# Windowed attention and channel mix on one core: every engine's order and engine choices re-planned, units 0 and 1's q and k loaded ahead

## The chip, the cores and the metric

The kernel runs on one core of a Trainium2 chip. The metric is the device time of one execution in microseconds (us). PE is the matrix engine, DVE the vector engine, ACT the scalar engine, POOL the GpSimd engine, and SP the engine whose queue issues nearly all DMAs here. Each of them works through its own list of instructions strictly in the order in which the program gave it; semaphores make an instruction wait for the work of another engine.

## What is computed

Two steps follow each other. First causal attention over 4 batches, 8 heads, 768 positions and 64 columns a head, where each position sees the 128 latest positions and the first 4 ("sinks"). Its result, with the heads put side by side (512 columns), is the x of an RWKV channel mix.

```python
keep = (pos[None, :] < 4) | ((rel >= 0) & (rel < 128))
a = softmax(where(keep, q @ k.T / 8, -1e9));  attn = a @ v
x = attn.transpose(0, 2, 1, 3).reshape(B, S, 512)
x_prev = x shifted by one position
xk = mu_k * x + (1 - mu_k) * x_prev
xr = mu_r * x + (1 - mu_r) * x_prev
kk = relu(xk @ w_k) ** 2              # 512 -> 1024
out = sigmoid(xr @ w_r) * (kk @ w_v)  # 1024 -> 512
```

All inputs and the output are float32. The kernel multiplies in bf16 and accumulates in float32.

## The kernel before, in words

The work is cut into 12 units of 256 positions: unit u is third `u % 3` of batch `u // 3`. For each unit these stages follow one another, each written as a few operations that one engine does:

- load (L281 to L341): two DMAs of 256 KB each for k, q and v. Those of v (L304), of k from unit 4 and of q from unit 8 on (L314) move rows of 256 bytes; k and q of the earlier units come in rows of 1 KB (L334). The weights come in five DMAs of 1 MB (L351).
- prepare (L514 to L690): a cast of k and q to bf16 (L533, L540; tiles `kb`, `qb`), then a transpose to `kt` and `qt`. k of units 4 to 11 and q of units 8 to 11 are transposed by a DMA of the SP queue (L559); the others on PE (L573), and ACT or DVE copies the result out of PSUM (L586). v is cast to `vb` (L643). The four keys that all positions see are set aside by POOL (`ksink`, L667) and by PE and DVE (`vsink`, L673, L677).
- attend: scores on PE (`sc`, L718), exponential on ACT (`e`, L772), mask by a DVE product (L786), values on PE (`o`, L805; the sink part L693, L700, L760), reciprocal and scaling on DVE (`rec` L819, `x` L822).
- mix (L831 on): x is transposed on PE and copied out (L846, L855), or for units 9 to 11 by a DMA (L866); DVE forms the difference to the position before (`td`, L874) and `xk` and `xr` (L885).
- ffn (L928 on): `xk @ w_k` on PE (L936), relu on ACT or DVE (L946, L950), square on ACT or DVE (L964, L960), `xr @ w_r` on PE with a tanh on ACT (L976, L982), `kk @ w_v` on PE (L994), the gate on DVE (L1003) and the store by SP (L1010). Of the last unit's second half the product and the store are cut in two (L906, L916, L921).

The weights are cast to bf16 in pieces of 128 by 1024 (L498, L502, L504).

None of this is scheduled by the compiler. `Plan.op` only records an operation with its engine; `Plan.run` (L172) then emits all of them in the order of a list of numbers, `ORDER`. Three tables were worked out ahead of time: `ORDER`, in which an entry of 0 or more is an operation and a negative one is a product of zeros into a spare PSUM bank (`P.fill`, L1014: it keeps PE at work and computes nothing); `CHOICE`, which for operations that can be done by several engines names one that is not the default; and `SLOTS`, which buffer of its pool each tile takes. Only the order within each engine counts, since the engines run side by side. The pools are small: three buffers each for raw k, q and v and for raw weights, four for `kt` and `qt`, two pairs of PSUM banks for scores and four single ones for everything else on PE. An operation on one engine that stands ahead of others and waits for a load or for a buffer holds up all that stand behind it on that engine, and a DMA on the SP queue that waits for its source holds up the loads behind it.

Of the kernel before, what the change touches and what calls it, by code (L numbers as in the profile page):

```python
# [18 lines left out]
    90: "ACT", 91: "ACT", 92: "ACT", 93: "ACT", 95: "ACT", 97: "ACT", 99: "ACT", 100: "DVE",  # L19
    103: "DVE", 108: "DVE", 109: "POOL", 111: "DVE", 112: "ACT", 113: "ACT", 139: "DVE", 142:  # L20
    "DVE", 144: "DVE", 145: "DVE", 148: "DVE", 151: "DVE", 154: "DVE", 196: "POOL", 199: "POOL",
    202: "POOL", 206: "DVE", 223: "DVE", 227: "DVE", 228: "ACT", 278: "DVE", 283: "DVE", 284:
    "POOL", 287: "ACT", 288: "DVE", 300: "DVE", 309: "ACT", 313: "ACT", 320: "DVE", 356: "DVE",
    358: "POOL", 363: "POOL", 366: "ACT", 367: "ACT", 369: "DVE", 389: "ACT", 446: "DVE", 447:
    "ACT", 527: "DVE", 548: "ACT", 552: "ACT", 555: "DVE", 560: "ACT", 595: "DVE", 597: "DVE",
    600: "POOL", 602: "DVE", 605: "ACT", 606: "DVE", 628: "ACT", 636: "ACT", 677: "POOL", 681:
    "DVE", 683: "DVE", 684: "DVE", 702: "ACT", 706: "ACT", 710: "ACT", 714: "ACT", 753: "DVE",
    759: "DVE", 761: "ACT", 782: "DVE", 783: "ACT", 787: "ACT", 791: "ACT", 795: "ACT", 832:
    "DVE", 838: "ACT", 839: "ACT", 859: "ACT", 866: "DVE", 867: "ACT", 906: "POOL", 912: "DVE",
    914: "ACT", 915: "DVE", 931: "ACT", 935: "ACT", 939: "ACT", 943: "ACT", 1000: "DVE", 1004:  # L30
    "DVE", 1005: "ACT", 1008: "DVE", 1009: "ACT", 1028: "DVE", 1037: "ACT",
# [116 lines left out]
class Plan:  # L148
# [23 lines left out]
    def run(self):  # L172
        keys = [(name, key) for o in self.ops for name, key in o["take"]]
        for (name, key), slot in zip(keys, SLOTS, strict=True):
            self.buf[key] = self.pools[name][slot]
# [8 lines left out]
def kernel(  # L184
# [14 lines left out]
    nc = tc.nc  # L199
# [14 lines left out]
    P = Plan()  # L214
# [854 lines left out]
```

## Time and profile before

| | |
|---|---|
| three runs | 167.48, 169.1 and 170.65 us, median 169.1 us |
| span of the profiled execution | 167.6 us |
| busy: PE, DVE, ACT, POOL | 159.7, 146.2, 133.4, 16.6 us |
| granted PE clock | full speed in every slice |
| bytes | 24.12 MB read from memory, 6.29 MB written |
| products of zeros | 44, the last three from 20.77 us on |
| last product on PE ends | 163.9 us |

The profile has no separate figure for the profiled execution beyond its span of 167.6 us, which lies 0.1 us above the fastest of the three runs and 1.5 us under their median. "Busy" of PE runs to the modelled end of each product, and products are pipelined: one of 512 columns is shown with some 380 ns, while in a row of four each takes 215 ns. So PE's share says when it had nothing at all, not how fast it went; the chain of waits shows the rows without the overlap. DVE and ACT overlap too, by less: a following instruction starts some 80 to 120 ns before the one ahead of it is shown to end.

### The profile page before, as it was taken

The numbers are of one execution on the slowest core, as the hardware profiler recorded it, in microseconds if no ns is written. First come the engines' busy times: TensorE is split into PE (matmuls) and PEld (weight loads), VectorE is DVE, ScalarE is ACT, GpSimd is POOL, SyncE is SP. The second block draws the span as 40 slices with busy tenths as digits, with TensorE's granted clock in tenths as the row PEclk, the third lists the DMA queues.
The fourth block names the chain that finished last, engine by engine and source line by source line (L and its number), as shares of the span: only waits on it lengthen the run. The fifth ranks groups of instructions, "written<-read, shape, count | busy, mean of one in ns | idle before, by whom it ended". The sixth has DMA issues, their size and how long they took to land.

```text
span 167.6 us, 4210 instructions
## 1 busy us (share of the span) xinstructions
PE 159.7 (95%) x1601; PEld 102.4 (61%) x1601; DVE 146.2 (87%) x375; ACT 133.4 (80%) x221; POOL 16.6 (10%) x43
## 2 busy tenths in 40 slices
PE   6999997999999999899999999999999999999991
PEld 1447574755558576676556885665765576764850
DVE  5189999999999999899999999989798799998821
ACT  4269998999999997999879999989799829614340
POOL 6423021005000010022000000010010000000000
PEclk9999999999999999999999999999999999999999
DMA  4999989999899999979999999999997774131303
GB/s 102 300 327 369 346 172 312 372 324 328 189 248 166 204 294 224 253 153 133 218 256 149 214 239 174 233 219 200 211 189 185 194 162 155 63 66 63 125 0 125
DMA packets 79042, 34.60 MB, mean 206 GB/s; under 512 B 67112, under 2 KB 73520, under 8 KB 79024
## 3 DMA queue, kind: packets, MB, share of 16 engines
q1 hardware_dynamic: 79008, 34.35, 92.0%
q8 instruction: 12, 0.20, 0.5%
q14 instruction: 6, 0.05, 0.1%
q10 hardware_dynamic: 16, 0.00, 0.0%
HBM read 24.12 MB, written 6.29 MB: 181 GB/s over the span
## 4 chain that ended last, share of the span: by engine, by line
PE 58%; DVE 11%; DMA 11%; SPq 7%; ACT 7%; issue 3%; ACTq 0%; DVEq 0%
PE bank L936 18%; PE bank L994 18%; PE bank L976 8%; DMA vs<-in_v_dram 6%; SPq L334 5%; PE sc L718 4%; PE bank L805 4%; DMA qs<-in_q_dram 3%; ACT e L772 3%; DMA qt<-qb 2%; DVE ob L1003 2%; DVE e L786 2%; PE bank L846 2%; DVE x L822 2%; PE bank L573 2%
## 5 line engine op out<-in xcount | busy, mean ns | idle before, releaser
L936 PE MATMUL bank<-xk,wk_sb 128*128 128x256 bf16 x384 | 48.1, 273 | 0.1
L994 PE MATMUL bank<-wv_h,kk 128*128 128x512 bf16 x184 | 46.4, 379 | 0.0
L772 ACT ACTIVATE e<-sc 128x1024 bf16<-128x1024 f32 (+1 forms) x48 | 45.4, 974 | 1.2 <-PE sc L718 1.2
L936 PEld LDWEIGHTS <-wk_sb 128*128 128x128 bf16 x384 | 36.2, 98 | 7.6 <-issue 0.7
L786 DVE TENSOR_TENSOR e<-e,mask 128x1024 bf16<-128x1024 bf16 (+1 forms) x48 | 30.7, 655 | 0.7 <-ACT e L772 0.5
L946 ACT ACTIVATE rl<-bank 128x512 bf16<-128x512 f32 x38 | 22.4, 616 | 8.6 <-PE bank L936 8.5
L994 PEld LDWEIGHTS <-kk 128*128 128x128 bf16 x184 | 16.6, 98 | 14.4 <-issue 0.3
L976 PE MATMUL bank<-wr_sb,xr 128*128 128x512 bf16 x96 | 23.8, 379 | 0.0
L885 DVE SCALAR_TENSOR_TENSOR xr<-td,mu_all,xt 128x256 bf16<-128x256 bf16 x48 | 22.5, 482 | 0.0
L885 DVE SCALAR_TENSOR_TENSOR xk<-td,mu_all,xt 128x256 bf16<-128x256 bf16 x48 | 21.3, 477 | 0.1
L964 ACT ACTIVATE kk<-rl 128x512 bf16<-128x512 bf16 x26 | 16.7, 649 | 5.3 <-DVE rl L950 5.3
L822 DVE TENSOR_TENSOR x<-bank,rec 128x256 bf16<-128x256 f32 x48 | 19.2, 416 | 0.3
L1003 DVE SCALAR_TENSOR_TENSOR ob<-th,bank 128x512 f32<-128x512 f32 x23 | 15.7, 681 | 4.2 <-PE bank L994 3.3
L805 PEld LDWEIGHTS <-e 128*128 128x128 bf16 x352 | 14.4, 97 | 5.8 <-DVE e L786 1.0
L805 PE MATMUL bank<-vb,e 128*128 128x65 bf16 x352 | 16.9, 193 | 0.8 <-DVE e L786 0.8
L982 ACT ACTIVATE th<-bank 128x512 f32<-128x512 f32 x24 | 14.3, 616 | 3.6 <-PE bank L976 3.5
L1014 PE MATMUL bank<-warm 128*128 128x512 bf16 x44 | 13.8, 440 | 1.5 <-DVE warm L1032 1.1
L718 PE MATMUL sc<-qt,kt 64*128 64x128 bf16 (+1 forms) x256 | 13.9, 237 | 0.3 <-DMA qt<-qb 0.2
L976 PEld LDWEIGHTS <-xr 128*128 128x128 bf16 x96 | 8.9, 98 | 8.6
L718 PEld LDWEIGHTS <-kt 64*128 64x128 bf16 x256 | 9.3, 94 | 4.5 <-issue 3.0
L874 DVE TENSOR_TENSOR td<-xt 128x512 bf16<-128x512 bf16 x24 | 10.1, 425 | 0.8 <-ACT xt L855 0.8
L855 ACT COPY xt<-bank 128x512 bf16<-128x512 bf16 x15 | 9.1, 608 | 1.8 <-PE bank L846 1.8
(72 smaller groups left out, 157.9 us busy)
## 6 DMA issues: line engine op xcount, KB each, us to landing
vs<-in_v_dram SPq DMA_DIRECT2D x24, 256.0 KB, 5.0
ks<-in_k_dram SPq DMA_DIRECT2D x24, 256.0 KB, 5.6
qs<-in_q_dram SPq DMA_DIRECT2D x24, 256.0 KB, 5.1
out_dram<-ob SPq DMA_DIRECT2D x23, 256.0 KB, 2.9
w<-in_moe_w_k_dram SPq DMA_DIRECT2D x2, 1024.0 KB, 7.3
w<-in_moe_w_v_dram SPq DMA_DIRECT2D x2, 1024.0 KB, 8.6
w<-in_moe_w_r_dram SPq DMA_DIRECT2D x1, 1024.0 KB, 7.1
kt<-kb SPq DMA_TRANSPOSE x16, 4.1
```

Source lines behind the costliest of these rows:

```text
L718: nc.tensor.matmul(out=sc[:, a, o0:o1], lhsT=lhs[rows], rhs=rhs[rows], start=u not in BIAS, stop=True, skip_group_check=u in BIAS)
L772: nc.scalar.activation(out=buf[ek][:, :, lo:], in_=buf[sck][:, :, lo:], func=AF.Exp, scale=scale)
L786: nc.vector.tensor_tensor(out=at, in0=at, in1=m, op=ALU.mult)
L805: nc.tensor.matmul(out=o[:, g, a, :], lhsT=e[:, a, e0:e0 + 128], rhs=rhs, start=(T == 0 and i == 0), stop=(i == len(blocks) - 1), skip_gro ...
L822: P.op("DVE", dve(256), lambda ok=ok, rk=rk, c=c: nc.vector.tensor_tensor(out=buf["x", u][:, :, 128 * c:128 * c + 128].rearrange("p g (a d ...
L885: nc.vector.scalar_tensor_tensor(out=buf[key][:, c, :], in0=buf[tk][:, i, :], scalar=mu[w][:, c:c + 1], in1=xt[:, c, t0 - 1:t0 + 255], op0 ...
L936: nc.tensor.matmul(out=ps[:, i, :], lhsT=wk_sb[:, c, 128 * f:128 * f + 128], rhs=xk[:, c, :], start=(c == 0), stop=(c == NC - 1), skip_gro ...
L946: nc.scalar.activation(out=buf[rk], in_=buf[psk].rearrange("p (i t) -> p i t", i=2), func=AF.Relu)
L964: nc.scalar.activation(out=buf["kk", u][:, 2 * f2:2 * f2 + 2, :], in_=buf[rk], func=AF.Square)
L976: nc.tensor.matmul(out=buf[psk], lhsT=buf["xr", u][:, c, 128 * g:128 * g + 128], rhs=wr_sb[:, c, :], start=(c == 0), stop=(c == NC - 1))
L994: nc.tensor.matmul(out=buf[psk], rhs=wv_h[:, f, :], lhsT=buf["kk", u][:, f, 128 * g:128 * g + 128], start=(f == 0), stop=(f == NF - 1))
L1003: P.op("DVE", dve(512), lambda psk=psk, tk=tk, bk=bk: nc.vector.scalar_tensor_tensor(out=buf[bk], in0=buf[tk], scalar=1.0, in1=buf[psk], o ...
```

## The change

The three tables are new, and the product of zeros can now be of two sizes. In the new `ORDER` the negative entries are all from -1 to -4, which stands for 512 columns as before, so the 128-column form is not used. There are 40 of them in place of 44.

```diff
 CHOICE = {
-    90: "ACT", 91: "ACT", 92: "ACT", 93: "ACT", 95: "ACT", 97: "ACT", 99: "ACT", 100: "DVE",
...
+    90: "POOL", 91: "ACT", 92: "POOL", 93: "POOL", 94: "POOL", 95: "POOL", 96: "ACT", 97: "ACT",
...
 ORDER = (
-    4, 80, 77, 0, 81, 79, 78, 82, 1, 2, 85, 3, 112, 84, 8, -1, -2, -3, -4, -1, -2, 88, 83, 6,
...
+    80, 81, 78, 77, 2, 79, 85, 82, 3, 103, -1, -2, -3, -4, -1, -2, -3, -4, -1, 104, 105, 109,
+    87, 110, 0, 1, 100, 106, -3, -4, -4, -1, 101, 107, 102, -1, -1, -1, 117, 123, 118, 111, 108,
...
 SLOTS = (
...
         for i in ORDER:
             if i < 0:
-                self.fill(self.pools["bank"][-1 - i])
+                self.fill(banks[(-1 - i) % len(banks)], 512 if -i <= len(banks) else 128)
             else:
                 self.ops[i]["emit"]()
...
-    P.fill = lambda bank: nc.tensor.matmul(out=bank, lhsT=warm[:, 0:128], start=True,
-                                           rhs=warm.unsqueeze(1).to_broadcast([128, 2, 256]),
-                                           stop=True)
+    def zeros(bank, n):
+        nc.tensor.matmul(out=bank[:, 0:n], lhsT=warm[:, 0:128], start=True, stop=True,
+                         rhs=warm.unsqueeze(1).to_broadcast([128, 2, 256]) if n == 512 else
+                         warm[:, 0:n])
+
+    P.fill = zeros
```

What the tables change, counted from the instructions of the two programs (L numbers of the kernel before):

| operation | DVE | ACT | POOL |
|---|---|---|---|
| cast of k, `kb` (L533, L540) | 6 to 5 | 15 to 2 | 3 to 17 |
| cast of q, `qb` (L533, L540) | 10 to 5 | 7 to 4 | 7 to 15 |
| cast of v, `vb` (L643) | 9 to 4 | 11 to 2 | 4 to 18 |
| casts of weights (L498, L502, L504) | 3 to 0 | 7 to 5 | 0 to 5 |
| `kt`, `qt`, `xt` out of PSUM (L586, L855) | 7 to 10 | 35 to 32 | |
| relu (L946, L950) | 10 to 11 | 38 to 37 | |
| square (L960, L964) | 22 to 11 | 26 to 37 | |

PE's real work, the DMAs and the stores are the same in kind and number. The SP queue's order begins, with the two halves of each: before v0 (first half), k0, q0, q1 (first half), k1, q1 (second half), q2 (first half), v0 (second half), q2, w_k first half, k2, w_k second half, k2, v1, v2 (first half), w_r, w_v, v2 (second half). After: q0, k0, v0, k1, q1, q2, k2, v1, k2, q2, v1 (k2, q2 and v1 with their halves interleaved), w_k, w_r, q3, k3, q3, v2, w_v, v3.

On PE, unit 1's attention now stands wholly ahead of unit 0's first product with w_k; before, 24 products with w_k stood between its scores and its values. Behind these first units PE's order is new too, mostly by a few places.

More of the change, by code (lines that the diff above doesn't have):

```diff
@@ L18 @@
 CHOICE = {
-    90: "ACT", 91: "ACT", 92: "ACT", 93: "ACT", 95: "ACT", 97: "ACT", 99: "ACT", 100: "DVE",
[L20 to L30, printed above, removed]
@@ L31 @@
-    "DVE", 1005: "ACT", 1008: "DVE", 1009: "ACT", 1028: "DVE", 1037: "ACT",
+    90: "POOL", 91: "ACT", 92: "POOL", 93: "POOL", 94: "POOL", 95: "POOL", 96: "ACT", 97: "ACT",
+    98: "ACT", 99: "ACT", 100: "DVE", 105: "DVE", 108: "DVE", 109: "POOL", 111: "DVE", 112:
+    "DVE", 113: "DVE", 139: "DVE", 142: "DVE", 148: "POOL", 193: "POOL", 196: "DVE", 199:
+    "POOL", 202: "DVE", 215: "DVE", 224: "ACT", 228: "ACT", 231: "DVE", 275: "POOL", 278:
+    "POOL", 281: "DVE", 283: "DVE", 284: "POOL", 288: "ACT", 293: "DVE", 309: "ACT", 313: "ACT",
@@ new lines @@
+    316: "DVE", 317: "ACT", 320: "DVE", 321: "ACT", 356: "POOL", 358: "POOL", 361: "POOL", 363:
+    "POOL", 369: "DVE", 385: "ACT", 388: "DVE", 389: "ACT", 393: "ACT", 397: "ACT", 436: "POOL",
+    438: "POOL", 440: "DVE", 441: "DVE", 443: "DVE", 456: "DVE", 473: "ACT", 516: "POOL", 518:
+    "POOL", 521: "POOL", 523: "POOL", 527: "DVE", 548: "ACT", 552: "ACT", 556: "ACT", 560:
+    "ACT", 595: "POOL", 597: "POOL", 600: "POOL", 615: "DVE", 628: "ACT", 632: "ACT", 636:
+    "ACT", 675: "POOL", 677: "POOL", 679: "POOL", 681: "POOL", 702: "ACT", 706: "ACT", 709:
@@ L32 @@
+    "DVE", 710: "ACT", 714: "ACT", 753: "POOL", 755: "POOL", 757: "POOL", 759: "POOL", 761:
+    "ACT", 783: "ACT", 786: "DVE", 787: "ACT", 791: "ACT", 795: "ACT", 830: "POOL", 834: "DVE",
+    838: "DVE", 855: "ACT", 859: "ACT", 862: "DVE", 863: "ACT", 867: "ACT", 906: "POOL", 908:
+    "DVE", 910: "POOL", 912: "POOL", 931: "ACT", 939: "ACT", 943: "ACT", 997: "ACT", 1000:
+    "DVE", 1004: "DVE", 1008: "DVE", 1009: "ACT", 1025: "ACT", 1028: "DVE", 1037: "ACT",
 }
@@ L175, in run @@
             self.buf[key] = self.pools[name][slot]
+        banks = self.pools["bank"]
         for i in ORDER:
             if i < 0:
-                self.fill(self.pools["bank"][-1 - i])
+                self.fill(banks[(-1 - i) % len(banks)], 512 if -i <= len(banks) else 128)
             else:
```

159 rows, old and new, of tables (ORDER, SLOTS) are left out of this document.

## Prediction

> **What bounds the kernel now.** I read the page's busy shares, then the same by stage, then the chain of waits for the price of each kind of work without the overlap, and last the timelines of the stages that the change touches.
>
> ```profile
> PE 159.7 (95%) x1601; PEld 102.4 (61%) x1601; DVE 146.2 (87%) x375; ACT 133.4 (80%) x221; POOL 16.6 (10%) x43
> ...
> DMA  4999989999899999979999999999997774131303
> ```
>
> Three engines and the DMAs are close to full together; POOL is nearly free. By stage (columns: stretch, length, busy of PE, PEld, DVE, ACT, POOL with their counts, clock, DMA share, GB/s):
>
> ```profile
> 0.00:21.40 21.40, 19.50 (x162) 10.08 (x163) 14.86 (x47) 14.06 (x21) 7.52 (x26) 1.00 0.96 288
> 21.40:30.40 9.00, 7.90 (x105) 5.74 (x104) 8.84 (x23) 8.30 (x14) 1.93 (x3) 1.00 0.92 256
> 30.40:164.00 133.60, 132.33 (x1339) 86.56 (x1336) 122.16 (x308) 111.04 (x188) 7.16 (x14) 1.00 0.94 192
> ```
> ```profile
> 30.00:60.00 30.00, 30.00 (x317) 19.44 (x312) 29.57 (x75) 29.69 (x52) 2.85 (x5) 1.00 1.13 257
> ```
>
> From 30.4 us PE hardly stops, but DVE and ACT are as full until 60 us. How much of PE's time is work? Counts from the groups of instructions, prices from the chain (start, length, what):
>
> ```profile
> L936 PE MATMUL bank<-xk,wk_sb 128*128 128x256 bf16 x384 | 48.1, 273 | 0.1
> L994 PE MATMUL bank<-wv_h,kk 128*128 128x512 bf16 x184 | 46.4, 379 | 0.0
> ...
> L976 PE MATMUL bank<-wr_sb,xr 128*128 128x512 bf16 x96 | 23.8, 379 | 0.0
> ...
> L805 PE MATMUL bank<-vb,e 128*128 128x65 bf16 x352 | 16.9, 193 | 0.8 <-DVE e L786 0.8
> ```
> ```profile
> 38.93 0.86 PE bank L994 x4
> 39.80 0.22 PE bank L846 x4
> ...
> 41.10 0.59 PE bank L805 x16
> ...
> 50.64 2.18 PE bank L936 x20
> ...
> 53.23 0.55 PE sc L718 x12
> ```
>
> 384 products at 0.109 (2.18/20) are 42 us, 280 at 0.215 (0.86/4) 60, 352 values at 0.037 13, 24 groups of scores at up to 0.55 some 12, 168 transposes at 0.055 9, the other 117 some 6: about 142 us of real work. The last product ends at 163.9 us, so 22 us are not work. By the same prices only 12 us were done at 30.4 us: 18 of the 22 are lost in the startup, 4 in all the rest. A change of order can win mostly there.
>
> **The change, part by part.**
>
> *Load order at the start.* The timeline of the startup (start, length, engine, line, count, wait before it):
>
> ```profile
> 8.59 0.43 DVE L540 CAST qb<-qs 128x512 bf16<-128x512 f32 x1 [1.66 <-DMA qs<-in_q_dram]
> ...
> 10.58 0.50 PE L718 MATMUL sc<-qt,kt 64*128 64x256 bf16 x8
> ```
> ```profile
> 17.90 1.11 ACT L498 ACTIVATE wk_sb<-w 128x1024 bf16<-128x1024 f32 x1
> ...
> 21.41 2.78 PE L936 MATMUL bank<-xk,wk_sb 128*128 128x256 bf16 x24
> ...
> 23.00 0.43 DVE L643 CAST vb<-vs 128x512 bf16<-128x512 f32 x1
> ...
> 30.42 3.81 PE L936 MATMUL bank<-xk,wk_sb 128*128 128x256 bf16 x32
> ```
>
> Half of v0 goes behind q0 and k0. A half is 256 KB, at the startup's 288 GB/s 0.9 us: the first scores start about 1.0 us earlier than 10.58 (0.6 to 1.3). The first half of w_k had 12 loads ahead of it and now has 16: 3.6 us later, so its cast starts near 21 instead of 17.90. v1, which DVE took at 23.00 behind both halves of w_k, now comes ahead of them, at about 17: unit 1's attention no longer waits for it. PE thus has other work to do until w_k is there, and unit 0's first products with w_k start some 2 to 3 us later than 21.41. What counts is how much work is done when PE becomes dense: the products at 30.42 are unit 1's first with w_k. They wait for `xk` from DVE, which in the stretch before is busy 8.84 of 9.00 us. Summing the instructions ahead of them on DVE with the prices of the chain,
>
> ```profile
> 25.35 1.01 DVE e L786
> ...
> 66.16 0.61 DVE ob L1003
> ...
> 82.95 0.33 DVE x L822
> 83.29 0.34 DVE qb L533
> ...
> 85.36 0.39 DVE xr L885
> ...
> 126.10 0.60 DVE e L786
> ```
>
> gives 20.1 us now and 19.4 after (fewer casts at 0.34). With 1.0 us of earlier start and 1.0 lost to POOL (below) they come 0.7 us earlier, and PE has 0.5 us more behind it by then. Startup: -1.2 us. If DVE did not bind, PE's own order and the loads would let them start near 28: -3. If POOL cost twice as much: 0.
>
> *36 casts of 512 columns and five of 1024 to POOL.* DVE gives up 1 `kb`, 5 `qb`, 5 `vb`, 11 squares at 0.34 and 3 weight casts at 0.6 (as `ob`): 9.3 us, and takes 3 copies and a relu, 2: -7.3 us. ACT gives up 31 casts, copies and a relu and takes 11 squares, net some 12 us at the 0.62 of a cast (row at 66.30 below). POOL takes over 22 us of 512-column casts (0.62) and some 6 of the larger ones, beside 16.6 busy now: 45 of 168 us, so POOL itself is not full. But POOL and DVE disturb each other:
>
> ```profile
> 71.55 1.17 DVE L960 TENSOR_TENSOR kk<-rl 128x512 bf16<-128x512 bf16 x2
> 71.69 0.75 POOL L533 CAST qb<-qs 128x512 bf16<-128x512 f32 x1 [9.97 <-PE bank L573]
> ```
> ```profile
> 25.02 0.81 POOL L643 CAST vb<-vs 128x512 bf16<-128x512 f32 x1
> ...
> 25.27 1.09 DVE L786 TENSOR_TENSOR e<-e,mask 128x1024 bf16<-128x1024 bf16 x1
> ```
> ```profile
> L786 DVE TENSOR_TENSOR e<-e,mask x48: 544/681/1097, 12.0 to 144.7; 128x1024 bf16<-128x1024 bf16 x32, 128x768 bf16<-128x768 bf16 x16
> ```
> ```profile
> L643 POOL CAST vb<-vs x4: 614/618/810, 23.9 to 111.6; 128x512 bf16<-128x512 f32 x4
> ```
>
> A mask takes 0.68 us, beside a cast 1.09; two squares take 1.17 where 0.76 would do; POOL's cast grows from 0.62 to 0.81. Of the 14 casts of now, five delay DVE (at 24.54, 25.27, 39.64, 71.88 and 111.90 us), by 0.34, three times 0.41, and 0.20: 1.8 us, 0.13 a cast. The price lies between 0 and 0.41 a cast (a large one twice that). I take 0.13, since DVE is as full now as it will be: 36 more small casts and 5 large ones are 46 such units, +6 us. DVE stays as loaded as it is (-7.3 + 6), ACT gets 12 us of air. On PE's end that is worth nothing in itself, as PE is full.
>
> The Trainium skill ("SBUF — State Buffer", section "Who interferes with whom") says that a DVE instruction with two SBUF inputs and a POOL instruction that reads SBUF exclude each other, and the later one is blocked until the other ends. The stretched rows agree; nine of 14 casts, which cost DVE nothing, show that it is not met each time. Were it met each time, the sum is that of the first rival.
>
> *Casts off ACT's and DVE's queues.* A cast that waits for its load holds up what stands behind it:
>
> ```profile
> 66.30 0.62 ACT L533 CAST kb<-ks 128x512 bf16<-128x512 f32 x1 [0.90 <-DMA ks<-in_k_dram]
> ...
> 67.95 0.43 DVE L874 TENSOR_TENSOR td<-xt 128x512 bf16<-128x512 bf16 x1 [0.80 <-ACT xt L855]
> ...
> 69.38 0.29 PE L693 MATMUL bank<-qt,ksink 128*32 128x256 bf16 x4 [0.59 <-ACT rl L946]
> ```
>
> A late k stops ACT 0.90, then DVE 0.80, then PE 0.59 us. With that cast on POOL this goes. Of the 4 us lost after 30.4 I take 0.5 off; ends: -2 (half the loss) and +2, since every order is new and could have such waits of its own.
>
> *DMAs.* Same transfers; the share is full to 126 us. Near the end PE waits for a transposed q:
>
> ```profile
> 127.46 3.35 DMA qt<-qb
> 130.82 0.04 issue
> 130.86 0.62 PE sc L718 x12
> ```
>
> This transpose is the 113th DMA of the SP queue, 1.16 us for each; in the new order unit 11's last one is the 115th (two transposes of x and a store more ahead of it, a load of v less), so 2.3 us later, 133.1, if nothing else changes, and about 1.5 us later if SP waits less on casts that POOL does at once. PE's order asks for it after 111 us of work instead of 108: from 132.3 there are 29.8 us of work left (32.5 now) and the same 0.6 lost, and PE ends at 162.7, -1.2 us (-0.4 with the 2.3). So the DMAs cap what the start can bring.
>
> *Zero products.* 40 instead of 44, all 512 wide: 0.9 us less on PE, inside waits for loads and for DVE: 0. If the cover is gone, each delays PE by 0.215. Four of them stand behind unit 0's first products with w_k: at worst +0.9.
>
> *Instruction fetches.* They take little of the DMAs, so counting them can move little:
>
> ```profile
> q8 instruction: 12, 0.20, 0.5%
> ```
>
> Sum: -1.2 at the start, -0.5 after, capped by the DMAs near -1.2: I take -1.3 us. From the last product to the end of the span (163.9 to 167.6) nothing changes. The profiled execution took 167.6, 1.5 under the median of 169.1; I put the difference on the median: 167.8 us.
>
> **The rivals.**
>
> 1. *POOL blocks DVE on most casts (slower).* At 0.41 a cast, the 17 small and 5 large ones of the first 60 us cost 11 us against 3 to 4 that DVE gives up by then and 1.2 of earlier start: DVE, full to 60 us, would be 6 us behind, and PE has no slack to recover: 175. It decides where a cast costs more than some 0.17; from 0.3 on the kernel is 2% slower (172.5). For it: three of five stretched rows show 0.41, and POOL will be busiest where DVE is fullest. Against: the mean of 0.13. By the skill's rule as read strictly, this one. 23%.
> 2. *New waits take the gain.* DMA lands unit 11's k 1 to 3 us later than reckoned because transposes wait on SP for POOL's casts, or orders untried so far stall PE as often as at 66 us: 169 to 170.5. 14%.
> 3. *DVE does not bind the start.* Unit 1's products with w_k start at 28, the casts cost POOL alone, and the SP queue, with kb cast as soon as it lands, saves the 2.3 us and more of its waits: -4, 165.1. For it: POOL is idle when k lands. 18%.
>
> **How the numbers follow.** The forecast (166.3 to 169) has 45%, 167.8 us. Range 164.5 to 172.5: it leaves out the worse half of rival 1 and the best end of rival 3. Faster by over 2% (under 165.7, about what a measurement of this kernel can tell from no change) is most of rival 3 and little of the forecast, 0.19; slower by over 2% (over 172.5) most of rival 1, 0.2; within it 0.61.
>
> **What the new profile would show.** First scores near 9.6 us; `vb` of unit 1 cast near 17; unit 1's first products with w_k at 29 to 30; DVE still above 95% from 30 to 60, with masks of 1.1 us beside POOL's casts, ACT below 90%; scores of unit 11 at 132 with a DMA as releaser. I am wrong if masks of 1.1 are the rule, or if PE's idle time after 30 us is above 6 us.

## The result, and the profile after

| | before | after |
|---|---|---|
| time, median (range) | 169.88 us (167.48 to 171.12, 4 runs) | 177.36 us (175.34 to 178.27, 4 runs) |
| ratio, 95% interval | | 1.047 (1.032 to 1.063) |
| span of the profiled execution | 167.6 us | 176.6 us |
| last product on PE ends | 163.9 us | 173.4 us |

The changed kernel is 4.7% slower. I had forecast 167.8 us, in a range to 172.5. (Ratios leave disturbed runs out; the slowest run of after, 178.27 us, is one of these and is the one that was profiled, so its trace shows about 1 us more than the 8 us of the ratio.) A time is 1.7 to 2.0 us longer than the span of the same execution in all runs that show both. So the profiled execution of before, with its span of 167.6 us, took some 169.4: the 1.5 us that I put between it and the median is this difference, and the forecast does not hang on it.

Rows of the page of after: busy times, the DMAs by slices, the chain that ended last; behind them the chain of before.

```profile
PE 159.3 (90%) x1597; PEld 102.2 (58%) x1597; DVE 152.0 (86%) x354; ACT 125.3 (71%) x201; POOL 49.4 (28%) x84
...
DMA  4999999699609488799799999999998763042313
...
PE 45%; DVE 36%; DMA 9%; issue 3%; SPq 3%; POOL 1%; ACT 0%; DVEq 0%; POOLq 0%
```
```profile
PE 58%; DVE 11%; DMA 11%; SPq 7%; ACT 7%; issue 3%; ACTq 0%; DVEq 0%
```

DVE has 21 instructions fewer than before and is busy 5.8 us longer: its instructions have become longer. Its share of the chain of waits goes from 11% to 36%. The DMAs, full to 126 us before, dip at 31 us and have holes from 44 us on. By stage (same columns as in the prediction):

```profile
0.00:21.40 21.40, 16.57 (x148) 8.28 (x149) 15.19 (x43) 12.15 (x19) 9.52 (x29) 1.00 0.91 269
21.40:30.40 9.00, 5.13 (x84) 3.75 (x85) 8.37 (x17) 8.35 (x13) 5.32 (x5) 1.00 1.09 343
30.40:60.00 29.60, 27.57 (x276) 19.15 (x276) 28.06 (x64) 23.69 (x39) 10.03 (x16) 1.00 0.76 200
30.40:173.40 143.00, 137.62 (x1367) 90.14 (x1366) 128.03 (x295) 104.83 (x170) 34.53 (x51) 1.00 0.78 178
```

From 21.4 to 30.4 us PE has 5.13 us of work where it had 7.90, and DVE does 17 instructions in the time of 23. Which instructions grew? Smallest, median and largest duration in ns of the two products behind `td`, before and after:

```profile
L885 DVE SCALAR_TENSOR_TENSOR xr<-td,mu_all,xt x48: 452/476/815, 18.8 to 156.8; 128x256 bf16<-128x256 bf16 x48
L885 DVE SCALAR_TENSOR_TENSOR xk<-td,mu_all,xt x48: 451/478/485, 19.2 to 153.4; 128x256 bf16<-128x256 bf16 x48
```
```profile
L889 DVE SCALAR_TENSOR_TENSOR xr<-td,mu_all,xt x48: 454/479/1252, 17.3 to 164.4; 128x256 bf16<-128x256 bf16 x48
L889 DVE SCALAR_TENSOR_TENSOR xk<-td,mu_all,xt x48: 456/481/1160, 17.9 to 164.0; 128x256 bf16<-128x256 bf16 x48
```

The medians are the same; the tail has grown. The timeline of after around the worst of them shows beside what they stand:

```profile
25.69 2.29 POOL L508 CAST wk_sb<-w 128x1024 bf16<-128x1024 f32 x2 [1.60 <-DMA w<-in_moe_w_k_dram]
25.82 1.25 DVE L878 TENSOR_TENSOR td<-xt 128x512 bf16<-128x512 bf16 x1
27.00 0.17 DVE L823 RECIPROCAL rec<-bank 128x4 f32<-128x4 f32 x1
27.09 1.56 DVE L889 SCALAR_TENSOR_TENSOR xk<-td,mu_all,xt 128x256 bf16<-128x256 bf16 x2
28.42 2.31 POOL L508 CAST wr_sb<-w 128x1024 bf16<-128x1024 f32 x2 [0.43 <-DMA w<-in_moe_w_r_dram]
28.57 1.25 DVE L889 SCALAR_TENSOR_TENSOR xr<-td,mu_all,xt 128x256 bf16<-128x256 bf16 x1
28.70 0.93 PE L940 MATMUL bank<-xk,wk_sb 128*128 128x256 bf16 x7 [1.16 <-DVE xk L889]
```

A `td` of 0.43 us takes 1.25 beside POOL's cast of a weight, and PE waits 1.16 us for the `xk` behind it.

Two sums of my own over the traces help to compare kernels. *DVE's stretch*: what each DVE instruction took beyond the shortest quarter of its own kind, where that is over 0.1 us. It is 1.8 us in 5 instructions before, 13.1 us in 33 after (20 `xk` and `xr`, 7 `td`, 5 masks, one cast). Each of the 33 overlaps a cast on POOL. *PE's loss* at a time: that time less the real work that PE has begun by then, at the prices of the prediction (141 us in all, counted product by product):

| PE's loss, us, at about | 20 | 30 | 60 | 100 | end |
|---|---|---|---|---|---|
| before | 13.9 | 18.1 | 19.1 | 21.2 | 22.8 |
| after | 15.4 | 20.0 | 25.0 | 27.2 | 32.4 |

Of the 9.6 us between the two, some 6 are lost by 60 us, and 3.6 behind 100 us.

### The profile page after: what moved, and what is told of

The parts are those of the page before. It is cut to its first block, busy times and chain, and to the rows that moved or that the text cites. A ratio compares the mean times of both kernels' runs of the same rounds, so it can differ in the third digit from the quotient of the medians.

```text
span 176.6 us, 4217 instructions
## 1 busy us (share of the span) xinstructions
PE 159.3 (90%) x1597; PEld 102.2 (58%) x1597; DVE 152.0 (86%) x354; ACT 125.3 (71%) x201; POOL 49.4 (28%) x84
## 4 chain that ended last, share of the span: by engine, by line
PE 45%; DVE 36%; DMA 9%; issue 3%; SPq 3%; POOL 1%; ACT 0%; DVEq 0%; POOLq 0%
PE bank L940 11%; PE bank L998 11%; DVE xk L889 8%; PE bank L980 7%; DVE e L790 6%; DVE xr L889 6%; PE bank L809 5%; DMA ks<-in_k_dram 5%; DVE td L878 4%; DVE x L826 4%; PE sc L722 4%; DVE ob L1007 2%; DMA out_dram<-ob 2%; PE bank L577 2%; PE bank L1019 2%
## 5 line engine op out<-in xcount | busy, mean ns | idle before, releaser
L776 ACT ACTIVATE e<-sc 128x1024 bf16<-128x1024 f32 (+1 forms) x48 | 44.3, 957 | 4.2 <-PE sc L722 4.1
L998 PE MATMUL bank<-wv_h,kk 128*128 128x512 bf16 x184 | 44.0, 379 | 0.0
L950 ACT ACTIVATE rl<-bank 128x512 bf16<-128x512 f32 x37 | 22.1, 598 | 21.5 <-PE bank L940 19.2
L790 DVE TENSOR_TENSOR e<-e,mask 128x1024 bf16<-128x1024 bf16 (+1 forms) x48 | 32.0, 677 | 1.0 <-ACT e L776 1.0
L889 DVE SCALAR_TENSOR_TENSOR xk<-td,mu_all,xt 128x256 bf16<-128x256 bf16 x48 | 25.8, 560 | 0.4
L889 DVE SCALAR_TENSOR_TENSOR xr<-td,mu_all,xt 128x256 bf16<-128x256 bf16 x48 | 25.4, 550 | 0.2
L968 ACT ACTIVATE kk<-rl 128x512 bf16<-128x512 bf16 x37 | 22.6, 630 | 0.5 <-DVE rl L954 0.3
L537 POOL CAST kb<-ks 128x512 bf16<-128x512 f32 x14 | 10.4, 748 | 42.4 <-DMA ks<-in_k_dram 42.3
L647 POOL CAST vb<-vs 128x512 bf16<-128x512 f32 x18 | 13.2, 736 | 18.8 <-DMA vs<-in_v_dram 16.6
L878 DVE TENSOR_TENSOR td<-xt 128x512 bf16<-128x512 bf16 x24 | 13.3, 552 | 1.3 <-DMA xt<-x 1.0
L722 PE MATMUL sc<-qt,kt 64*128 64x128 bf16 (+1 forms) x256 | 13.9, 238 | 0.0
L1019 PE MATMUL bank<-warm 128*128 128x512 bf16 x40 | 11.7, 421 | 1.1 <-DVE warm L1039 1.1
## 6 DMA issues: line engine op xcount, KB each, us to landing
w<-in_moe_w_k_dram SPq DMA_DIRECT2D x2, 1024.0 KB, 10.5
```

The lines of the kernel that those rows point to most:

```text
L722: nc.tensor.matmul(out=sc[:, a, o0:o1], lhsT=lhs[rows], rhs=rhs[rows], start=u not in BIAS, stop=True, skip_group_check=u in BIAS)
L776: nc.scalar.activation(out=buf[ek][:, :, lo:], in_=buf[sck][:, :, lo:], func=AF.Exp, scale=scale)
L790: nc.vector.tensor_tensor(out=at, in0=at, in1=m, op=ALU.mult)
L878: P.op("DVE", dve(512, 0.5), lambda cs=cs, tk=tk: nc.vector.tensor_tensor(out=buf[tk], in0=xt[:, cs, t0:t0 + 256], in1=xt[:, cs, t0 - 1:t0 ...
L889: nc.vector.scalar_tensor_tensor(out=buf[key][:, c, :], in0=buf[tk][:, i, :], scalar=mu[w][:, c:c + 1], in1=xt[:, c, t0 - 1:t0 + 255], op0 ...
L950: nc.scalar.activation(out=buf[rk], in_=buf[psk].rearrange("p (i t) -> p i t", i=2), func=AF.Relu)
```

## The experiments

Theories: A, POOL's casts stretch DVE's instructions, and PE waits for them; B, the new order of loads at the start starves PE; C, the new order has waits of its own later. Differences in us are ratios times 169.4, about the median of before in all comparisons.

**Old order with new choices, new order with old choices.** The edit of choice_only puts the new `CHOICE` into the kernel before; order_only puts the old one into the changed kernel.

> The old order and buffers with the new engine choices (56 casts on POOL). Theory A: the loss is there without the new order, 174 to 178 us, DVE stretched by 10 to 13 us. Theories B and C: the choices cost little by themselves, 168 to 171.5 us.

174.9 us, ratio 1.037 (1.030 to 1.044): 6.3 us are lost without the new order (8 with it). DVE's stretch is 9.6 us in 26 instructions.

> The new order and buffers with the engine choices of the kernel before (POOL 14 casts instead of 56). Theory A (POOL's casts stretch DVE, 0.23 us each, 13 us in all, and PE waits for DVE): most of the loss goes, 168 to 171 us, DVE stretched by some 2 us. Theory B (the new order of loads and lists up to 35 us loses some 5 us there, whoever casts): 173 to 176 us, PE's loss at 40 us stays near 23 us. Theory C (the new order behind 40 us has waits of its own, some 5 us): 172 to 175 us.

238 us, at a granted clock of 0.877. No theory had this. The old choices put casts that wait for their loads on ACT at places of an order that was made for POOL; the list of waits has, for ACT alone,

```profile
ACT vb L644 <- DMA vs<-in_v_dram: 19.7, 4, 8.7
```

(us in total, times, longest). So this run tells nothing of B and C, only that an order and its choices cannot be taken apart. The same holds, in small, for choice_only.

**Spare casts alone.** Three extra POOL instructions behind each of the 14 casts of the kernel before; all else stays.

```diff
                 self.ops[i]["emit"]()
+                if i in EXTRA:
+                    for _ in range(3):
+                        self.extra()
...
+    P.extra = lambda: nc.gpsimd.tensor_copy(out=spare_b, in_=spare)   # burst_casts
+    P.extra = lambda: nc.gpsimd.memset(spare, 0.0)                    # burst_writes
```

> The kernel before with three spare casts of 512 float32 columns to bf16 (constant source, unused target) on POOL behind each of its 14 casts: 42 more, as many as the change adds, nothing else moved. Theory A: 42 times 0.23 to 0.28 us more DVE time, of which the part in the full stretches reaches PE: 173 to 178 us. Theories B and C: POOL has room, 169.5 to 171.5 us.

175.5 us, ratio 1.041 (1.035 to 1.048); stretch 10.8 us in 31 instructions. POOL is busy 28% of the time, and that is enough to lose 7 us.

> As burst_casts, 42 extra POOL instructions in threes behind POOL's casts of the kernel before, but each only writes (zeros into an unused tile of 640 float32 columns, about 0.65 us, as long as a cast) and reads nothing. Theory A, if what DVE waits for is POOL's reading: DVE stretched by some 2 us as in the kernel before (10.8 with the casts), 169 to 170.5 us. If instead the 6 us of burst_casts come from POOL's own casts being late behind the bursts: 174 to 176 us again.

170.1 us, ratio 1.007 (1.002 to 1.011): 1.1 us in place of 7. The bursts are nearly as long (42 instructions of 652 ns; those of casts were 753), so POOL's own casts are nearly as late; what is gone is the reading. DVE's stretch is 4.4 us in ten instructions, where I had expected some 2: five have two inputs, the other five are casts of DVE. A piece of its timeline shows both sides:

```profile
71.37 0.73 POOL L539 CAST qb<-qs 128x512 bf16<-128x512 f32 x1 [7.54 <-DMA qs<-in_q_dram]
71.55 1.17 DVE L966 TENSOR_TENSOR kk<-rl 128x512 bf16<-128x512 bf16 x2
72.05 1.31 POOL L1026 MEMSET spare<- 128x640 f32 x2
72.64 0.47 DVE L891 SCALAR_TENSOR_TENSOR xr<-td,mu_all,xt 128x256 bf16<-128x256 bf16 x1
...
76.54 2.33 POOL L1026 MEMSET spare<- 128x640 f32 x3
77.37 0.16 DVE L825 RECIPROCAL rec<-bank 128x4 f32<-128x4 f32 x1
77.45 0.85 DVE L546 CAST qb<-qs 128x512 bf16<-128x512 f32 x1
```

Beside a cast the squares are stretched; beside POOL's filling `xr` takes its 0.47. Over the trace 30 DVE instructions with two inputs from SBUF (`xk`, `xr`, `td`, masks, squares) meet fillings alone for over 0.15 us, and none is stretched; the five that are stretched all meet one of the 14 real casts. DVE's own casts (one input, 0.42 us) are stretched by fillings as well: the 0.85 here, and two others, which are all that meet fillings alone for over 0.15 us. The Trainium skill ("SBUF — State Buffer", section "Who interferes with whom") says just this: two SBUF inputs on DVE contend with a POOL instruction that reads SBUF and not with one that only writes, and a DVE cast can enter a mode that takes the shared pair of ports whole. The trace agrees in both points.

**The changed kernel without POOL's reading.** The casts on POOL read 4 columns, so that they still wait for their load, and then fill the target with zeros; the values are left out of the result. For 512 columns the two take 0.29 + 0.53 us on average, against 0.74 of a cast in after.

```diff
+    def write_only(out, in_):
+        nc.gpsimd.tensor_copy(out=out[..., 0:4], in_=in_[..., 0:4])
+        nc.gpsimd.memset(out, 0.0)
...
-                       "POOL": (600.0, cast(nc.gpsimd.tensor_copy), True)},
+                       "POOL": (600.0, cast(write_only), True)},
```

> The changed kernel, but POOL's casts read 4 of 64 columns (of w: 4 of 256 or 512) and then fill the whole target with zeros, so that order, waits for loads and POOL's busy time stay about the same and its reading goes; the values are left out of the result. Theory A: DVE stretched by 3 to 6 us in place of 13, 169 to 173 us. Theory B (the new order of loads and lists loses 5 us up to 35 us): what it loses there stays, 174 to 176; theory C: 176 to 177.5 us.

172.1 us, ratio 1.012 (1.002 to 1.021): 6 of the 8 us go with the reading, and stretch falls from 13.1 to 0.7 us. The largest `xk` now is near the median:

```profile
L893 DVE SCALAR_TENSOR_TENSOR xr<-td,mu_all,xt x48: 456/479/486, 17.5 to 158.7; 128x256 bf16<-128x256 bf16 x48
L893 DVE SCALAR_TENSOR_TENSOR xk<-td,mu_all,xt x48: 456/479/488, 17.9 to 158.3; 128x256 bf16<-128x256 bf16 x48
```

PE's loss is 18.1 us at 30 and 19.5 at 60, as in the kernel before: theory B falls for this order, though w_k is nearly as late as in after (first cast at 22.55 and 23.05 us). What is left arises behind 100 us: 21.4 us there, 26.4 at the end. So of the two parts of after's loss the one by 60 us goes with the reading, and the one behind 100 us stays.

> The kernel before with its 14 casts on POOL only writing (the values are left out of the result): what reading costs it already. DVE was stretched by 1.8 us; at three quarters of it, as in burst_casts and choice_only, 1.3 us less: 167.7 to 168.2 us. If the tiny casts and fills are as dear as casts or later: 169 to 170, and then the 171.8 of choice_write_only contains such a cost too.

168.3 us, ratio 0.992 (0.987 to 0.996): reading costs the kernel before 1.4 us too. So the stand-in is not dear, at least for 14 casts, and the fair comparison of the two kernels without POOL's reading is 1.012 to 0.992: 2.0%, or 3.4 us (by the two intervals give or take some 1%). The added reading thus costs 4.6 of the 8 us, and 3.4 have another cause. Whether the stand-in, a little longer than a cast, costs something when it stands for 55 of them was not tried; such a cost would be part of the 3.4.

> The old order with the new engine choices (174.9 us), POOL's casts only writing (the values are left out of the result). What DVE and ACT gain by giving up casts then stands alone, without POOL's reading. Theory A with my prediction's credit (7.3 us less work on DVE counts against its stretch): 166 to 168 us. Theory A without credit (the casts that DVE gave up were not what PE waited for): 169 to 170.5 us. If the choices cost something beside the reading: 171 to 174.

171.8 us, ratio 1.018 (1.011 to 1.025). Against before_write_only the choices lose 4.5 us by themselves, most of it between 30 and 60 us (PE's loss at 30: 18.3 against 17.1, at 60: 22.5 against 18.8). DVE and ACT have their casts off, nothing stretches them (0.0 us), and no time is won. So the air that DVE and ACT get is worth nothing in this order. The chain of waits names the place: from 33 to 43 us it runs on ACT alone, which is busy 9.98 of these 10 us, while DVE is busy 6.51 (9.10 in before_write_only). Four casts of w_v are on ACT there; in before_write_only two of them are on DVE. So the time set free is on the wrong engine in this stretch.

**Half of the choices.** The new entries of `CHOICE` from operation 430 on, the old ones before.

> The old order; the new choices only for operations behind about 55 us (k of unit 5 and all that is recorded after it), the old ones ahead: some 30 more POOL casts. Theory A: loss in proportion where DVE has little room (by 60 us the kernel with all new choices had lost 4.0 us on PE, behind that 2.1): 171 to 172.5 us. If POOL's casts cost only in the first 60 us: 169 to 170 us.

172.4 us, ratio 1.017 (1.010 to 1.024), stretch 8.0 us: the new choices cost in the later stages as well. How much of these 2.9 us is POOL's reading and how much the choices themselves, this run does not part.

**The weights' casts back to ACT and DVE** (operations 90, 92, 93, 95 on ACT, 94 on DVE).

> The changed kernel with the five weight casts of 1024 columns taken off POOL again, put on the engines of the kernel before (four on ACT, one on DVE). Theory A: 5 large casts are 10 of the 66 units of POOL's work, in the stretch where DVE sets the pace: 1.5 to 3 us less, 174.5 to 176 us. A form of theory B in which POOL's slow casts of w_k and w_r (1.04 to 1.23 us each, one behind the other) hold up unit 0's and unit 1's products: 3 to 5 us less, 172.5 to 174.5. Theory C: no change, 177.

180.1 us, ratio 1.067 (1.061 to 1.072): against every theory, it is slower than the changed kernel. The timeline names the wait:

```profile
27.77 0.69 DVE L508 CAST wr_sb<-w 128x1024 bf16<-128x1024 f32 x1 [6.96 <-DMA w<-in_moe_w_r_dram]
```

DVE stands 7 us before a weight that has not landed, and PE 7.4 us for a mask behind it. In this order these casts are better on POOL, contention included.

**The order of loads alone,** in the kernel before: `2, 3, 0, 1, 4, 5, 6, 7, 8, 9, 19, 17, 12, 18, 20, 13, 10, 11, 14, 21` in place of the first 20 loads.

> The kernel before with the changed kernel's order of the first 20 loads alone (q0, k0, v0, k1, q1, q2, k2, v1, then w_k 3 to 4 loads later). My prediction's reason (first scores 1 us earlier, w_k later but not waited for): 168 to 169.5 us. Theory B, that the later w_k starves PE: 171 to 174 us, since this kernel's order still puts 24 products with w_k ahead of unit 1's values.

173.4 us, ratio 1.028 (1.018 to 1.038). w_k is cast 5.3 us later, and the products follow:

```profile
23.19 1.11 ACT L498 ACTIVATE wk_sb<-w 128x1024 bf16<-128x1024 f32 x1
...
26.71 2.78 PE L936 MATMUL bank<-xk,wk_sb 128*128 128x256 bf16 x24
```

The old order of PE needs w_k early, as B says; the new one has unit 1's attention in between, and write_only shows it loses no more than 1 us by 30 us.

**Late waits undone.** In after POOL stands before unit 11's k, with `vb` of unit 9 behind it; PE waits 0.66 us for that `vb`.

```profile
126.06 0.62 POOL L537 CAST kb<-ks 128x512 bf16<-128x512 f32 x1 [13.92 <-DMA ks<-in_k_dram]
...
128.23 0.61 POOL L647 CAST vb<-vs 128x512 bf16<-128x512 f32 x1
```

late_fix moves three entries of `ORDER`: load 64 behind 63, cast 906 behind 762, store 803 ahead of 879.

> The changed kernel with three late places of its order undone: the load of v's second half of unit 9 right behind the first half (11 DMAs earlier), POOL's vb and ksink of unit 9 ahead of the cast of unit 11's k that waits 14 us for its load, and the store of unit 7's first half ahead of that of unit 8's second half. Theory C (late order): the waits of PE at 128 us (0.8 us) and 146 us (1.2 us) go, 175 to 176.3 us against 177.4. If these waits are only the place where a loss made earlier shows, or are replaced by the next load's: 177 to 178.

177.2 us, ratio 1.050 (1.041 to 1.059): nothing.

> The same three places undone in the variant whose POOL casts only write (172.1 us; the values are left out of the result). Contention and late order together are then the whole loss: 168.5 to 170.5 us. If something else of the order costs 2 to 3 us: 171 to 172.5.

171.9 us, ratio 1.016 (1.006 to 1.026): nothing either. The waits of PE in write_only and in write_only_late_fix:

```profile
122.53 0.28 PE L813 MATMUL bank<-vb,e 128*128 128x65 bf16 x4 [1.28 <-POOL vb L254]
...
141.34 0.29 PE L768 MATMUL bank<-vsink,es 64*128 64x130 bf16 x4 [0.71 <-DVE ob L1011]
```
```profile
128.73 0.29 PE L701 MATMUL bank<-qt,ksink 128*32 128x256 bf16 x4 [0.56 <-DMA qt<-qb]
136.03 0.27 PE L768 MATMUL bank<-vsink,es 64*128 64x130 bf16 x3 [0.65 <-DVE x L830]
141.29 0.29 PE L768 MATMUL bank<-vsink,es 64*128 64x130 bf16 x4 [0.80 <-DVE ob L1011]
```

The wait of 1.28 us is gone, and a transposed q that a DMA brings is 0.56 us late in its place.

**SP's standing still.** In after SP stops for 3.7, 3.8 and 4.9 us between 43 and 62 us, before a transpose whose cast is late and two stores; in the kernel before there is nothing of the kind on stores in this stretch. Theory D: the DMA time lost here comes back as late loads behind 100 us. stores_later moves the loads of unit 5's k and unit 4's v (35, 36, 33, 34) ahead of these waits, and store 329 behind load 50; six_outs has six output buffers besides.

> The changed kernel with SP's queue mended between 43 and 62 us, where it stood 12.4 us waiting in three places while the DMAs had air: loads of unit 5's k and unit 4's v ahead of the transposes and stores that wait (store of unit 0's first half 4 loads later, that of unit 1's first half 10 DMAs later). Theory D (POOL's casts make DVE late, late outputs and casts stop SP's in-order queue, and the DMA time lost there comes back as late loads behind 100 us): PE's loss from 90 us on (5.2 us, 1.7 in the kernel before) shrinks, 174 to 176 us against 177.4. If the DMAs' lost time does not reach PE: 177 to 178.

> The same mended SP queue in the variant whose POOL casts only write (172.1 us; the values are left out of the result). Theory D: its remaining 2 to 3 us over the kernel before arise behind 100 us from late transfers: 169.5 to 171 us. If they do not come from SP's waits between 43 and 62 us: 172.

183.8 us, 1.087 (1.078 to 1.097), and 179.8 us, 1.066 (1.057 to 1.075): slower by 7 and 9 us than after and write_only. My moved store holds the buffer that DVE's next output needs, and PE stops for 7.7 us:

```profile
76.04 1.87 PE L940 MATMUL bank<-xk,wk_sb 128*128 128x256 bf16 x8 [7.72 <-DVE ob L1007]
```

> As stores_later, with six buffers for the outputs in place of three, so that a later store makes no output product on DVE wait (in stores_later DVE and then PE waited 8 us for the store that I had moved). Theory D: SP's 12 us of standing still between 43 and 62 us gone without a new wait, 174 to 176 us against the changed kernel's 177.4. If DMA time lost there does not reach PE: 177 to 178.

> As write_only_stores_later, with six output buffers (POOL's casts only write, the values are left out of the result). Theory D: 169.5 to 171 us. If the 2 to 3 us above the kernel before do not come from SP's waits there: 172.

182.9 us, 1.084 (1.076 to 1.093), and 177.5 us (174.1 to 178.7, no ratio). The buffers took that wait away, but SP now stands from 55.3 to 64.9 us before the next transpose, since DVE casts that half of k at 64.46:

```profile
54.66 0.63 SPq L342 DMA_DIRECT2D qs<-in_q_dram  x1
64.94 1.21 SPq L567 DMA_TRANSPOSE kt<-kb  x1
```

So SP never ran free in these four, and theory D was not put to the test. It stays open.

**Single repairs of the kernel before.** k6_on_pool adds `521: "POOL"`; wv_later moves load 15 two loads later besides.

> The kernel before with one cast moved: the second half of unit 6's k, which makes ACT wait 0.9 us for its load at 66.3 us, on POOL instead of ACT. By my prediction's term for casts off ACT's queue this stall of PE (0.59 us) goes: 168.4 to 168.8 against 169.1. If the next late thing takes its place or the cast costs DVE 0.4 us: 169.0 to 169.5.

168.6 us, ratio 0.998 (0.994 to 1.003).

> The kernel before with the cast of unit 6's second half of k on POOL, and on SP the load of w_v's first half two loads later (it waits 3.6 us for a buffer at 23 us and holds up the loads behind it). If SP's wait costs the end of the kernel something: 167 to 168.3 us. By the trace of before, where PE loses 4 us in all behind 30 us, no more than 1 us is there to be had: 168.3 to 169.5.

169.8 us, ratio 1.001 (0.996 to 1.006). Neither can be told from no change. No version here that computes everything beats the kernel before.

## Why the prediction was wrong, point by point

*Load order.* Half right. First scores 9.13 us (10.58 before; I said 1.0 earlier, it is 1.45), `vb` of unit 1 at 16.33 (I said 17). w_k was mis-sized: its first cast starts at 23.05, not 21. I had counted loads as if they came one by one; the page gives 10.5 us from issue to landing for w_k's halves (7.3 before), where a half alone at the startup's 288 GB/s would take 3.6, so they share the DMAs with their neighbours. Unit 0's first product with w_k comes at 27.28 us (I said 23.5 to 24.5), unit 1's at 34.36 in place of 29 to 30; in write_only that one is at 30.93. That DVE binds the start was right, and so it was DVE's stretch that went into PE's start.

*36 casts and five to POOL*: the step that failed, in two terms. First the price, "0.13 a cast", "since DVE is as full now as it will be". It measured (13.1 - 1.8) / 46 units = 0.25 us in after, (9.6 - 1.8) / 46 = 0.17 in choice_only and (10.8 - 1.8) / 42 = 0.21 in burst_casts. A hit costs 0.40 us (13.1 / 33), as my rows had said; what I had wrong is how often it comes. In the kernel before 5 of 14 casts delayed DVE, in after 38 of 55 (33 instructions). Those 14 stood where that order had put them, and were no sample of what 41 others would meet. Second the credit, "DVE stays as loaded as it is (-7.3 + 6)". choice_only gives DVE the 7.3 us and loses 6.3 us; burst_casts gives it nothing and loses 7; and choice_write_only has the credit without any stretch: 4.5 us lost against before_write_only, none won. A sum of busy time does not set off one against the other: the casts that DVE gave up were not what PE waited for, while the stretch falls on `td`, `xk`, `xr` and masks, which PE does wait for. The 4.6 us that the added reading costs belong to these two terms. The rest of the sum had nothing but gains, and without the reading 3.4 us were lost: a second miss, under DMAs below.

*Rival 1* is thus the mechanism of the larger part: 38 of 55 casts on POOL overlap a stretched instruction of DVE (5 of 14 before), and the kernel is slower by over 2%. Its rate (0.41) and its threshold (0.17) were off, and masks of 1.1 us, which I had named as its mark, are not the rule (mean 677 ns against 655): the tail of `xk`, `xr` and `td` shows it.

*Casts off ACT's and DVE's queues.* weights_off_pool shows the mechanism, larger than I had it: 7 us of DVE's wait for one weight. But moving the one cast behind the stall at 66 us, which I had priced at 0.59 us, brought no gain clear of noise (k6_on_pool: 0.3 us, by its interval between 1.1 won and 0.5 lost).

*DMAs.* Unit 11's scores came at 141.44 us, not 132.3, and PE did not stand waiting for a DMA there; in write_only they came at 135.07. In write_only the chain of waits behind 100 us runs for 18% of the time through loads of k and a store of the output, in before_write_only through PE alone. That is *rival 2* in kind, new waits for transfers, and it goes with the 3.4 us that are lost without any reading. Which of the late transfers is the root, or what makes them late, stays open: undoing three of them (late_fix) won nothing, and the runs on SP's queue did not isolate it.

*Zero products and instruction fetches* were not tried. PE's idle time behind 30.4 us is 143.0 - 137.6 = 5.4 us, below the 6 us that I had set as a mark of error: a bad mark, since "busy" of PE runs on over gaps between pipelined products.

## What to carry to other kernels

An idle engine is not free if its reading holds up a full one: price such a move by what the neighbour's instructions may become (here +0.4 us for each hit, with 5 of 14 casts hitting before and 38 of 55 after), and look at the tail of durations, not at the mean. Work taken off an engine pays only if another engine waited for it; of a delay of what others do wait for a good part comes back (9 us of stretch cost 7 in burst_casts, 12.5 cost 6 between after and write_only, 9.6 cost 3.2 between choice_only and choice_write_only). To test contention, keep the instruction and take away only its reading; to test an order, don't mix it with choices made for another.

## What the runs showed of the hardware

POOL's filling (no reading) cost DVE's instructions with two SBUF inputs nothing in 30 meetings of burst_writes, while it stretched DVE's own float32 casts by 0.33 to 0.43 us in three of three. For two inputs it counts where they lie: in after, of 50 DVE instructions with two inputs from SBUF that overlapped a POOL cast by over 0.15 us, 32 were stretched; of 16 with one of the two from PSUM (`x`, `ob`, `vsink`), none. POOL is delayed as well: its casts of 512 columns, from 0.61 us, have a mean of 0.74 in after and 0.75 in the bursts. In order_only the granted clock was 0.50 from 30 to 47 us, where PE was busy 1.8 of 17 us, and 0.877 over the whole span.
